# A transformer block with modulated layer norms: first loads in another order, low parts of h from a fused product, six weight slices prepared sooner

## The chip, the cores and the metric

The kernel runs on one core of one Trainium2 chip. A core has five engines that each work through their own instructions in order and wait for each other by semaphores: TensorE (PE in the profile; PEld is its weight load), VectorE (DVE), ScalarE (ACT), GpSimd (POOL) and SyncE (SP), which here only issues DMA transfers. The metric is the device time of one execution in microseconds (us).

## The reference

x is 2048 rows of 512 numbers. A conditioning vector c gives six vectors by one product; the block is attention with 32 heads of 16, then a dense layer with the Mish activation, each behind a layer norm that is scaled and shifted by such vectors.

```python
mod = (_silu(c) @ w_mod).reshape(c.shape[0], 6, 1, -1)
sa, ca, ga, sb, cb, gb = (mod[:, 0], mod[:, 1], ...)
h = _layernorm(x, axis=-1) * (1 + ca) + sa
x = x + ga * _A_ref(h, A_wqkv, A_wo)      # qkv, softmax(q k^T * 16**-0.5) v, @ wo
h = _layernorm(x, axis=-1) * (1 + cb) + sb
x = x + gb * _B_ref(h, B_w1, B_b1, B_w2)  # (h @ w1 + b1) -> mish -> @ w2
```

All is float32. The kernel gets this precision from products in a rounded format (fp32r): it splits each operand into a high part, which is its rounded copy, and a low part, which is what the rounding left, and adds three products: high by high, high by low, low by high.

## The kernel before, in words

**Stages.** In the first stage (about 50 us) the rows of x are read in 16 tiles of 128 rows, four of them a block (`tb`, 512 rows). Each tile is normalised, transposed by TensorE, and scaled and shifted by the columns `modc` into h, kept as `h_h` (high) and `h_l` (low). For each block the first slice of keys (128 columns, eight heads) is computed and put into DRAM, for block 0 that of the queries too, and for blocks 0 and 1 four of the 16 tiles of values. In the second stage (20 steps with t below 0, `PRO`) TensorE computes the maxima of the scores of the first iteration, with further units of q, k and v between them. The attention loop follows: 32 iterations of 16 steps. The last block of the dense layer closes the program.

**What sets the order.** The code is written in the order in which each engine is to work; nothing reorders it. Work that belongs to no step is hung on half-steps: `at(h, f)` runs f at half-step h, where step t has the half-steps 2t and 2t + 1, so that h = -40 is the first. All loads and puts go through SP's queue in that order.

**The first loads.** SP issues c, then the two parts of w_mod that are needed at once (1 MB each: columns for sa and ca), then x tiles 0 to 3, a key and a query slice of `wqkv`, x tiles 4 to 7, a value slice, the other x tiles. Meanwhile GpSimd fills tiles: `sel`, `vq`, `zer`, the five `qa`, and `ka[0]` and `ka[1]`, whose rows of ones stay beside the keys.

**The modulation.** `sil` = c / (1 + exp(-c)) is computed in four small steps, on ScalarE and VectorE. Eight products of `sil` with w_mod (L449) give four partial rows for each of sa and ca in one PSUM bank, which ScalarE copies (L453); 16 products with `sel` (L455) add the partial rows and turn them into columns. VectorE writes them to `modc` (L463, L464).

**The first block's norm.** `first_norm` has VectorE compute statistics of four tiles (L395, L396) and GpSimd the scales in two pairs (L397 to L400). `first_apply` normalises tiles 0 to 2 on ScalarE (L418), 3 on VectorE (L420). `split_hi` and `split_lo` split the first key and query slices.

**A block's h.** `tr_tb` transposes (L435; for block 0 `first_tr`, L427), and for each of four parts k of 128 columns ScalarE writes `h_h` from PSUM (L440), VectorE computes the same value unrounded into `hf` (L441) and `h_l` is hf less h_h (`lo_sub`, L101): on VectorE for the k in `LOV[tb]`, on GpSimd for the others. `stats_tb` and `apply_tb` are the norm of later blocks (L374 to L385). `hi_copy` and `lo_sub` (L94 to L101) are helpers, so many splits share these lines.

**The early weight slices.** `early_prep` loads one of 14 slices of w1 into `ep`, splits it on GpSimd (L98, L101) and puts both parts into `w1scr` in DRAM, for six of the slices in the second stage. They are read in the dense layers.

## Time and profile before

| | us |
|---|---|
| median of 3 runs | 1690.67 |
| lowest, highest run | 1689.92, 1690.83 |
| the profiled execution | 1691.02 |
| its span, first to last instruction | 1689.2 |
| first stage, to the first maxima (L553) | 50.3 |
| second stage, 20 steps, to the first step of the loop (L588) | 51.5 |
| from there to the end of the span | 1587.3 |

TensorE's granted clock is 1.00 on the mean. The busy time of an engine is an average over stages with different limits: the table's first rows concern 50 of 1689 us, and how the engines share them is read from the timeline of that stretch. A row of the chain of waits has a start, a length and what the time went to. A row of the timeline has a start, a length, the engine, the line, the operation, what it writes and reads, and in brackets how long the engine was idle before it and who released it. `x4` means four instructions in one row.

### The profile page before, as it was taken

How to read it: one execution, taken by the hardware profiler on the slowest of the kernel's cores; microseconds unless marked ns; L12 is line 12 of the kernel's file. 1: busy time of each engine (PE TensorE's matmuls, PEld its weight loads, DVE VectorE, ACT ScalarE, POOL GpSimd, SP SyncE). 2: the span in 40 equal slices, each digit the busy share in tenths (PEclk: the TensorE clock that was granted, in tenths of full speed). 3: DMA queues.
4: the chain of work that ended last, by engine and by line, in shares of the span. 5: the costliest groups of instructions: out<-in, count | busy, mean ns of one | idle time of the engine just before them, and what ended most of it. 6: DMA issues, size and time to landing. Idle time of an engine off the chain costs nothing.

```text
span 1689.2 us, 33772 instructions
## 1 busy us (share of the span) xinstructions
PE 1667.3 (99%) x12418; PEld 921.5 (55%) x12418; DVE 1441.5 (85%) x2369; ACT 1355.1 (80%) x2612; POOL 821.1 (49%) x843
## 2 busy tenths in 40 slices
PE   7999999999999999999999999999999999999999
PEld 5755655555444455555555455555555455555687
DVE  8898888888989988888889888888889888883377
ACT  6257777777778998888888998888888998889674
POOL 7555224655313564556323564556323565555442
PEclk9999999999999999999999999999999999999999
DMA  7877556777755443434355434534354533533261
GB/s 248 269 244 199 147 150 185 218 223 216 231 142 146 110 94 98 117 88 129 84 137 152 115 77 93 139 77 127 87 144 122 130 94 77 144 107 132 75 230 63
DMA packets 115406, 238.98 MB, mean 141 GB/s; under 512 B 24928, under 2 KB 50544, under 8 KB 109288
## 3 DMA queue, kind: packets, MB, share of 16 engines
q1 hardware_dynamic: 115240, 236.82, 49.9%
q8 instruction: 98, 1.61, 0.4%
q14 instruction: 68, 0.56, 0.1%
HBM read 180.48 MB, written 51.45 MB: 137 GB/s over the span
## 4 chain that ended last, share of the span: by engine, by line
PE 91%; DVE 3%; ACT 3%; DMA 2%; POOL 1%; issue 1%; SPq 0%; ACTq 0%; DVEq 0%; POOLq 0%
PE bk L606 29%; PE ring L588 22%; PE ring L539 20%; PE bk L139 11%; PE bk L132 3%; PE ring L1219 2%; PE ring L132 2%; DVE mx L541 2%; ACT pr L591 1%; PE ring L553 0%; DMA qa<-mt 0%; DMA xt<-in_A_x 0%; PE ring L922 0%; DMA kscr<-qh 0%; PE ring L568 0%
## 5 line engine op out<-in xcount | busy, mean ns | idle before, releaser
L541 DVE TENSOR_REDUCE mx<-ring 128x1 f32<-128x512 f32 x1968 | 1223.1, 682 | 150.0 <-PE ring L539 136.4
L591 ACT ACTIVATE pr<-ring 128x512 f32<-128x512 f32 x2048 | 1078.4, 603 | 207.1 <-PE bk L139 124.7
L539 PE MATMUL ring<-ka,qa 64*128 64x512 f32 x1968 | 817.9, 429 | 1.4 <-ACT pr L591 1.1
L588 PE MATMUL ring<-qa,ka 64*128 64x512 f32 x2048 | 759.1, 402 | 3.4 <-ACT pr L591 1.9
L606 PE MATMUL bk<-pr,vg 128*32 128x512 f32 x4096 | 545.1, 604 | 0.0
L539 PEld LDWEIGHTS ring<-ka,qa 64*128 64x128 f32 x1968 | 350.5, 184 | 326.2 <-DVE mx L541 251.3
L588 PEld LDWEIGHTS ring<-qa,ka 64*128 64x128 f32 x2048 | 373.7, 184 | 194.7 <-DVE mx L541 111.4
L139 PE MATMUL bk<-h,w 64*128 64x512 f32 (+1 forms) x1080 | 278.1, 390 | 0.0
L139 PE MATMUL bk<-w,a_h 64*128 64x512 f32 x632 | 210.9, 413 | 0.0
L139 PEld LDWEIGHTS bk<-h,w 64*128 64x128 f32 x1080 | 178.5, 184 | 9.3 <-ACT pr L591 1.5
L606 PEld LDWEIGHTS bk<-pr,vg 128*32 128x32 f32 x4096 | 81.2, 108 | 135.4 <-issue 126.0
L139 PE MATMUL bk<-w,a_l 64*128 64x512 f32 x316 | 124.0, 392 | 0.0
L139 PEld LDWEIGHTS bk<-w,a_h 64*128 64x128 f32 x632 | 106.8, 184 | 4.3 <-ACT hb L800 1.0
L978 POOL TENSOR_TENSOR y<-yd,y 128x512 f32<-128x512 f32 x44 | 56.9, 1293 | 89.0 <-ACT yd L977 79.7
L812 POOL TENSOR_SCALAR qq<-ee 128x512 f32<-128x512 f32 x25 | 15.5, 619 | 169.6 <-ACT ee L806 169.6
L828 POOL TENSOR_TENSOR qq<-qq,rr 128x512 f32<-128x512 f32 x42 | 54.1, 1289 | 85.9 <-ACT rr L822 85.9
L814 POOL TENSOR_TENSOR hb<-hb,ee 128x512 f32<-128x512 f32 x42 | 54.1, 1288 | 79.6 <-DVE ee L810 77.7
L139 PE MATMUL bk<-w,o_hl 64*128 64x512 f32 x288 | 79.1, 405 | 0.0
L101 POOL TENSOR_TENSOR a_l<-hb,a_h 128x512 fp32r<-128x512 f32 x53 | 73.1, 1379 | 4.4
L98 POOL TENSOR_SCALAR qh<-qf 128x512 fp32r<-128x512 f32 x27 | 16.7, 619 | 90.8 <-ACT qf L262 69.4
L139 PEld LDWEIGHTS bk<-w,a_l 64*128 64x128 f32 x316 | 58.3, 185 | 3.4
L139 PE MATMUL bk<-h_h,wl 64*128 64x512 f32 x168 | 57.2, 420 | 0.2 <-ACT pr L591 0.2
(219 smaller groups left out, 1909.1 us busy)
## 6 DMA issues: line engine op xcount, KB each, us to landing
ka<-kscr SPq DMA_DIRECT2D x124, 384.0 KB
w<-w2scr SPq DMA_DIRECT2D x56, 512.0 KB
w<-w1scr SPq DMA_DIRECT2D x46, 512.0 KB
vg<-vscr SPq DMA_DIRECT2D x32, 552.0 KB
qa<-qscr SPq DMA_DIRECT2D x124, 100.0 KB
kscr<-qh SPq DMA_DIRECT2D x16, 512.0 KB
qscr<-qh SPq DMA_DIRECT2D x32, 256.0 KB
w2scr<-hl SPq DMA_DIRECT2D x14, 512.0 KB
```

Source lines behind the costliest of these rows:

```text
L101: (nc.gpsimd if eng == "p" else nc.vector).tensor_sub(lo, src, hi.bitcast(F32))
L132: nc.tensor.matmul(acc, l, r, start=start, stop=stop)
L139: i = nc.tensor.matmul(acc, l[64 * g:64 * g + 64], r[64 * g:64 * g + 64], start=start and not then, stop=bool(stop and then))
L539: nc.tensor.matmul(pm, qt[64 * s:64 * s + 64, qs * P:(qs + 1) * P], kt[64 * s:64 * s + 64, kb * TB:(kb + 1) * TB], start=True, stop=True)
L541: nc.vector.tensor_reduce(out=mxs[n][:, s, 4 * j + qs, kb:kb + 1], in_=pm, op=ALU.max, axis=AX.X)
L588: nc.tensor.matmul(p_, kt[64 * s:64 * s + 64, kc * P:(kc + 1) * P], qt[64 * s:64 * s + 64, :], start=True, stop=True)
L591: e = nc.scalar.activation(pr, p_, AF.Exp, scale=SCALE)
L606: nc.tensor.matmul(accs[n][32 * h:32 * h + 32, :], vgs[n][:, o:o + 32], pts.pop((t, h)), start=(kc == 0), stop=(kc == 15))
L814: (nc.vector if tail else nc.gpsimd).tensor_mul(hb, hb, ee)
L828: nc.gpsimd.tensor_mul(qq, qq, rr)
L978: nc.gpsimd.tensor_add(y[i], yd, y[i])
L1219: nc.tensor.matmul(po[i // 2][:, i % 2, :], l[:, s], w[:, r, :], start=(f == 0 and j == 0), stop=(f == FT - 1 and j == 2))
```

## The change

**First loads.** c is loaded through ScalarE's queue. On SP the x tiles 0 to 3 come first, then the first part of w_mod in four tiles of 128 rows, the key slice, the second part in four tiles, the query slice, and the rest as before. SP's queue before (`wma` is w_mod, `xt` a tile of x, `wr` a slice of wqkv):

```order
L332 DMA cc_129<-in_c 128x4x1
L342 DMA wma0_131<-in_w_mod 128x4x512
L342 DMA wma1_132<-in_w_mod 128x4x512
L337 DMA xt_135<-in_A_x 128x512
L337 DMA xt_137<-in_A_x 128x512
L337 DMA xt_139<-in_A_x 128x512
L337 DMA xt_141<-in_A_x 128x512
L234 DMA wr_143<-in_A_wqkv 128x4x128
```

and now:

```order
L333 DMA xt_133<-in_A_x 128x512
L333 DMA xt_135<-in_A_x 128x512
L333 DMA xt_137<-in_A_x 128x512
L333 DMA xt_139<-in_A_x 128x512
L340 DMA wma00_125<-in_w_mod 128x512
L340 DMA wma01_126<-in_w_mod 128x512
L340 DMA wma02_127<-in_w_mod 128x512
L340 DMA wma03_128<-in_w_mod 128x512
L232 DMA wr_145<-in_A_wqkv 128x4x128
L340 DMA wma10_129<-in_w_mod 128x512
```

The x tiles stand ahead of all of w_mod, and the key slice between its two parts.

**Fills, sums and spare transposes.** `sel` is gone; ScalarE fills `ka` from a column of ones. The sums over w_mod are accumulated in PSUM over the four parts of c (`mod_sums`), the row is copied by VectorE and one transpose makes the columns (`mod_cols`). `keep_busy` issues transposes of the identity whose result nobody reads: 40 at the start, 6, 2 after each of four sums, and 4. The norm of the first eight tiles goes by pairs (`stats_two`); tile 3 is normalised by GpSimd.

**Low parts of h.** `hf` is now one fused operation, PSUM times the scale less h_h, and `h_l` is hf plus the shift column. In block 0, VectorE makes the low parts of k = 2 and 3 in place of k = 1. VectorE's instructions before, from the last statistic of block 1:

```order
L375 BN_AGGR ln_mv_246<-ln_st 128x2
L441 TENSOR_SCALAR hf<-ring,modc 128x512
L441 TENSOR_SCALAR hf<-bk,modc 128x512
L101 TENSOR_TENSOR h_l<-hf,h_h 128x512
L441 TENSOR_SCALAR hf<-ring,modc 128x512
L441 TENSOR_SCALAR hf<-bk,modc 128x512
L374 BN_STATS ln_st<-xt 128x6
```

and now:

```order
L401 BN_AGGR ln_mv_359<-ln_st 128x2
L459 SCALAR_TENSOR_TENSOR hf<-ring,modc,h_h 128x512
L459 SCALAR_TENSOR_TENSOR hf<-bk,modc,h_h 128x512
L459 SCALAR_TENSOR_TENSOR hf<-ring,modc,h_h 128x512
L462 TENSOR_SCALAR h_l<-hf,modc 128x512
L459 SCALAR_TENSOR_TENSOR hf<-bk,modc,h_h 128x512
L462 TENSOR_SCALAR h_l<-hf,modc 128x512
L99 TENSOR_TENSOR wl<-wr,wh 128x1024
L381 BN_STATS ln_st<-xt 128x6
```

Two low parts stand there in place of one, and the value slice's low part (`wl`), which came after the four statistics of block 2, comes ahead of them.

**Early slices.** The six slices start at half-steps -39, -37 to -29 in place of -37, -34 to -22; each is split 4 half-steps after its load in place of 7, and put 7 after in place of 10. GpSimd before (`ep` a slice, `wl` the low part of a weight slice, `qh` the high part of a query unit):

```order
L98 TENSOR_SCALAR ep_791<-ep_790 128x512
L101 TENSOR_TENSOR ep_790<-ep_790,ep_791 128x512
L101 TENSOR_TENSOR wl_915<-wr_639,wh_914 128x512
L98 TENSOR_SCALAR ep_827<-ep_826 128x512
L101 TENSOR_TENSOR ep_826<-ep_826,ep_827 128x512
L98 TENSOR_SCALAR qh_945<-qf_947 128x512
```

and now:

```order
L96 TENSOR_SCALAR ep_817<-ep_816 128x512
L99 TENSOR_TENSOR ep_816<-ep_816,ep_817 128x512
L96 TENSOR_SCALAR ep_846<-ep_845 128x512
L99 TENSOR_TENSOR ep_845<-ep_845,ep_846 128x512
L96 TENSOR_SCALAR ep_878<-ep_877 128x512
L99 TENSOR_TENSOR ep_877<-ep_877,ep_878 128x512
L99 TENSOR_TENSOR wl_1014<-wr_728,wh_1013 128x512
```

All six splits now stand ahead of that weight slice's low part; before, it came after four.

The diff, cut to its core:

```diff
-    LOV = ((1,), (), (1, 3), (1, 3))
+    LOV = ((2, 3), (), (1, 3), (1, 3))
...
+    cc = cst.tile([P, DK], F32, name="cc")
+    nc.scalar.dma_start(cc, c.rearrange("o (k p) -> p (o k)", p=P))
...
+        wma = [[lp.tile([P, D], F32, name=f"wma{i}{k}") for k in range(DK)] for i in range(2)]
+        def load_mod(i):
+            for k in range(DK):
+                nc.sync.dma_start(wma[i][k], w_mod[k * P:(k + 1) * P, i * D:(i + 1) * D])
...
         for t in range(4):
             load_x(t)
+        load_mod(0)
         slice_load(1, 0, lp, lp)
+        load_mod(1)
         slice_load(0, 0, lp, lp)
...
-        for i in range(2):
-            nc.gpsimd.memset(ka[i].bitcast(F32), 1.0)
+        hi_copy("a", ka[0], ones.to_broadcast([P, S]))
...
+        def keep_busy(n):
+            for _ in range(n):
+                nc.tensor.transpose(spare[:, :P], ident, ident)
+        keep_busy(40)
...
+        def mod_sums(i, ks):
+            for k in ks:
+                for m in range(DK):
+                    nc.tensor.matmul(prs[i][32 * m:32 * m + 32, :P], sil[:, k:k + 1].to_broadcast([P, 32]),
+                                     wma[i][k][:, m * P:(m + 1) * P], start=(k == 0), stop=(k == DK - 1))
...
+        def mod_cols(i):
+            row = lp.tile([P, P], F32, name=f"row{i}")
+            nc.vector.tensor_copy(row, prs[i][:, :P])
+            nc.tensor.transpose(prs[i][:, P:2 * P], row, ident)
+            cols = prs[i][:, P:2 * P:32]
...
-                nc.vector.tensor_scalar(hf, pt, modc[:, 1, k:k + 1], modc[:, 0, k:k + 1], op0=ALU.mult, op1=ALU.add)
-                lo_sub("v" if k in LOV[tb] else "p", h_l[:, k, s], hf, h_h[:, k, s])
+                nc.vector.scalar_tensor_tensor(hf, pt, modc[:, 1, k:k + 1], h_h[:, k, s].bitcast(F32), op0=ALU.mult,
+                                               op1=ALU.subtract)
+                if k in LOV[tb]:
+                    nc.vector.tensor_scalar_add(h_l[:, k, s], hf, modc[:, 0, k:k + 1])
+                else:
+                    nc.gpsimd.tensor_add(h_l[:, k, s], hf, modc[:, 0, k:k + 1].to_broadcast([P, TB]))
...
+        for q in range(2):
+            stats_two(q)
+        first_apply(3, "p")
+        mod_sums(0, (0, 1))
+        keep_busy(6)
+        first_apply(0)
+        first_tr(0)
+        mod_sums(0, (2,))
+        first_apply(1)
+        first_tr(1)
+        mod_sums(0, (3,))
+        first_apply(2)
+        first_tr(2)
+        first_tr(3)
+        mod_cols(0)
+        hi_k = split_hi(1, 0, "a")
+        split_lo(1, 0, hi_k, "v")
+        for k in range(DK):
+            mod_sums(1, (k,))
+            keep_busy(2)
+        mod_cols(1)
+        keep_busy(4)
+        hi_q = split_hi(0, 0, "p")
+        split_lo(0, 0, hi_q, "p")
+        for q in range(2, 4):
+            stats_two(q)
+        tr_tb(0, pts=pts)
+        for i in range(4, 8):
+            first_apply(i)
+            if i == 5:
+                slice_split(2, 0, eng="v")
...
-        at(h + 7, split)
-        at(h + 10, put)
+        at(h + 4, split)
+        at(h + 7, put)
...
-        at(3 * i - 37, lambda i=i: early_prep(i, 3 * i - 37))
+        at(2 * i - 39, lambda i=i: early_prep(i, 2 * i - 39))
```

102 lines of the change are left out of this document (33 added, 69 removed).

## The prediction

> **What bounds the kernel now.** I read the page first, then the chain of waits in order of time, then the timeline of the first 52 us engine by engine. The page's busy row and its shares of the chain:
>
> ```profile
> PE 1667.3 (99%) x12418; PEld 921.5 (55%) x12418; DVE 1441.5 (85%) x2369; ACT 1355.1 (80%) x2612; POOL 821.1 (49%) x843
> PE 91%; DVE 3%; ACT 3%; DMA 2%; POOL 1%; issue 1%; SPq 0%; ACTq 0%; DVEq 0%; POOLq 0%
> ```
>
> TensorE carries 91% of the chain. Nothing in the diff changes the attention loop's own instructions, so a gain can only be a shift: the loop starts sooner and the rest follows at the same pace. The chain shows where the start is not TensorE's (start us, us, what):
>
> ```profile
> 2.31 7.47 DMA xt<-in_A_x
> ...
> 9.79 0.70 DVE ln_st L395
> ...
> 22.95 2.22 ACT xt L385 x3
> ...
> 38.04 4.52 PE ring L132 x29
> ...
> 48.72 1.15 DVE h_l L101
> ...
> 49.91 0.50 PE ring L132
> ...
> 51.07 1.86 PE bk L132 x14
> ```
>
> Up to 9.8 us the program waits for the first row tiles of x; until 23 us it is VectorE, GpSimd and ScalarE that prepare block 0 and 1; from 30 to 45 us ScalarE and TensorE take turns, and VectorE's last low part at 49.87 lets TensorE go. At 50.4 the maxima of the scores begin. From there to the loop's first step (50.34 to 101.88), busy time by engine:
>
> ```profile
> 50.34:101.88 51.54, 51.42 (x299) 36.64 (x298) 47.57 (x44) 9.84 (x22) 29.74 (x28) 1.00 0.88 280
> ```
>
> TensorE is busy 51.42 of 51.54 us there. So I ask one question: how much sooner does that stretch begin?
>
> **The change part by part. First, the start.** Rows of the timeline (start, us, engine, line, operation), and one of the table of stages (GB/s at the end):
>
> ```profile
> 1.52 0.48 POOL L78 MEMSET sel<- 1x1 f32 x4
> ...
> 3.17 0.20 ACT L361 ACTIVATE sil_e<-cc 128x4 f32<-128x4 f32 x1 [1.18 <-DMA cc<-in_c]
> 3.41 5.33 DVE L362 TENSOR_SCALAR sil_e<-sil_e 128x4 f32<-128x4 f32 x1 [1.76 <-ACT sil_e L361]
> 5.16 3.56 POOL L358 MEMSET ka<- 128x2048 f32 x2
> ...
> 14.82 0.60 ACT L94 CAST wh<-wr 128x512 fp32r<-128x512 f32 x1
> ...
> 25.07 1.04 ACT L94 CAST wh<-wr 128x1024 fp32r<-128x1024 f32 x1
> ```
> ```profile
> 4.00:5.00 1.00, 0.00 (x0) 0.00 (x0) 1.00 (x1) 0.00 (x0) 1.00 (x3) 1.00 1.04 406
> ```
>
> VectorE's addition for the SiLU takes 5.33 us on 512 numbers: it ends at 8.74, just as GpSimd's fills end at 8.72. The change takes the two ka fills (3.56) and the sel fills (0.48) off GpSimd, so its fills end near 4.7. ScalarE fills ka instead; by 0.60 for 512 columns and 1.04 for 1024, 2048 cost 0.60 + 3 x 0.44 = 1.9. ScalarE was free at 1.99 (3.17 less 1.18); with the issue of c ahead of it (some 0.4) the exponential runs near 4.4. The addition, the reciprocal and the product then end near 5.2.
>
> The x tiles now go first. At 406 GB/s four tiles (1.05 MB) take 2.6 us instead of following 2.1 MB of w_mod (5.2 us); x0 is there near 4.1 and x3 near 6.0. So the statistics, which stand behind the SiLU on VectorE, begin at 5.25 instead of 9.79. The steps behind them:
>
> ```profile
> 11.59 0.19 POOL L397 TENSOR_SCALAR ln_rs<-ln_mv 128x2 f32<-128x2 f32 x1 [2.88 <-DVE ln_mv L396]
> ...
> 12.81 0.19 POOL L400 TENSOR_TENSOR ln_rs<-ln_rs 128x2 f32<-128x2 f32 x1
> ```
>
> A pair's scales take 1.41 (11.59 to 13.00), four statistics 3.2 to 3.3 (below: 16.66 to 19.88), one normalisation about 0.8. Second pair: 5.25 + 3.3 + 0.1 + 1.41 = 10.1, normalised 10.9.
>
> TensorE then has eight transposes, four groups of sums for 1 + ca with two spare transposes each, and one transpose of the sums. Its rows, cold and warm:
>
> ```profile
> 9.21 3.64 PE L449 MATMUL ring<-wma,sil 128*32 128x512 f32 x16 [9.21 <-DVE sil L364]
> ...
> 17.11 0.42 PE L427 MATMUL ring<-ident,xt 128*128 128x128 f32 x1
> ...
> 20.98 0.63 PE L132 MATMUL ring<-h_h,wl 128*128 128x512 f32 x1
> ...
> 22.84 0.39 PE L132 MATMUL ring<-h_h,wl 128*128 128x512 f32 x1
> ...
> 25.39 0.60 PE L435 MATMUL bk<-ident,xt 128*128 128x128 f32 x4
> ```
>
> The same product takes 0.63 at 20.98 and 0.39 at 22.84, a transpose follows the next after 0.21 at 17 us and after 0.11 at 25: TensorE runs at half pace until about 21.5. Before, eight products of 512 columns took 3.64, 0.455 each; a group of four with 128 columns is one such, 0.455 cold and 0.23 warm. I take warm, because 40 spare transposes fill it from 1.4 us on. Eight transposes end at 12.0, four times 0.23 + 0.22 makes 13.9, and the copy, the transpose and the addition (0.25, 0.3, 0.15, each between two neighbours of its size) and their hand-overs make 14.75. By then all of w_mod that is needed has landed: 3.4 MB at 406 GB/s from 2.9, and 0.5 to be seen, is 11.8. Before, VectorE was past that point at 16.66: **1.9 sooner**.
>
> **Then VectorE**, whose next 11 us have no gap before:
>
> ```profile
> 16.66 0.68 DVE L374 BATCH_NORM_STATS2 ln_st<-xt 128x6 f32<-128x512 f32 x1
> ...
> 19.88 0.81 DVE L441 TENSOR_SCALAR hf<-ring,modc 128x512 f32<-128x512 f32 x1
> 20.61 0.80 DVE L441 TENSOR_SCALAR hf<-bk,modc 128x512 f32<-128x512 f32 x1
> ...
> 26.70 1.21 DVE L101 TENSOR_TENSOR wl<-wr,wh 128x1024 fp32r<-128x1024 f32 x1
> 27.82 0.81 DVE L441 TENSOR_SCALAR hf<-ring,modc 128x512 f32<-128x512 f32 x1
> ...
> 29.26 1.28 DVE L101 TENSOR_TENSOR ql<-ring,qh 128x512 fp32r<-128x512 f32 x2
> ```
>
> Before: 27.82 - 16.66 = 11.16 to block 1's first hf. Now the same statistics twice (2 x 3.22), the weight's low part (1.12), four fused products and two low parts in place of one. A fused product reads PSUM and SBUF as ql does: between 0.62 (1.28 for two) and 0.73 (hf to hf); I take 0.62, the row with its operands, 2.5 for four. The new low part, an addition of one tensor with a column, has one relative, the normalisation on VectorE:
>
> ```profile
> 15.04 2.68 POOL L101 TENSOR_TENSOR wl<-wr,wh 128x512 fp32r<-128x512 f32 x2
> 15.12 1.48 DVE L420 TENSOR_SCALAR xt<-xt,ln_rs 128x512 f32<-128x512 f32 x1 [2.03 <-POOL ln_rs L400]
> ```
> ```profile
> L101 DVE TENSOR_TENSOR h_l<-hf,h_h 128x512 fp32r<-128x512 f32 x5 | 5.8, 1167 | 0.2
> ```
>
> It ended at 16.60, 0.2 after the first of GpSimd's two operations (15.04 + 1.34): about 0.25 of its own and a wait to the end of what GpSimd has begun. So it costs 0.25 to 1.5, and the subtraction that it replaces 0.69 to 1.17 (the mean). GpSimd works on the low parts of k = 0 and 1 at that time; not knowing to 0.5 us where in a 1.3 us operation VectorE asks, I take half of it: 2 x (0.25 + 0.65) = 1.8. Sum 6.44 + 1.12 + 2.5 + 1.8 = 11.86, so block 1's first hf comes at 26.6, 1.2 sooner.
>
> [...] Both waits taken to the operation's end on my schedule (0.85 and 0.8 rather than 0.65) would be an estimate of 1688.4 for the whole.
>
> **Then GpSimd**, whose four low parts of block 1 TensorE needs:
>
> ```profile
> 29.43 5.06 POOL L101 TENSOR_TENSOR h_l<-hf,h_h 128x512 fp32r<-128x512 f32 x4
> ...
> 34.79 1.18 PE L132 MATMUL ring<-h_l,wh 128*128 128x512 f32 x4
> ...
> 35.28 0.19 POOL L376 TENSOR_SCALAR ln_rs<-ln_mv 128x4 f32<-128x4 f32 x1 [0.79 <-DVE ln_mv L375]
> ...
> 36.94 1.27 POOL L101 TENSOR_TENSOR h_l<-hf,h_h 128x512 fp32r<-128x512 f32 x1
> ```
>
> Scales 1.7 (35.28 to 36.94), four low parts 5.06. An addition with a column spread over 512 has no row; between the 0.62 of a one-tensor operation on GpSimd's queue and these 1.27, I take 1.27, the same two-operand form. 26.6 + 0.1 + 1.7 + 5.06 = 33.5. Before it was 34.49, and TensorE came only at 34.79. Now TensorE comes first: ScalarE's normalisations of x4 to x7 end near 21.9 (was 25.2), the transposes and late products follow, and by the old distances TensorE stands there at 32.4. It gets the last part at 33.5 and ends at 34.0 instead of 35.97: **1.95 sooner**. ScalarE and TensorE then alternate as before (38.04 becomes 36.1).
>
> **The last block.**
>
> ```profile
> 48.04 1.26 POOL L101 TENSOR_TENSOR h_l<-hf,h_h 128x512 fp32r<-128x512 f32 x1 [1.95 <-DVE hf L441]
> ```
>
> The last low part ended at 49.87, 0.57 after GpSimd's at 49.30. The new one ends 0.25 after it, which saves 0.3; the same on k = 1 saves 0.3 ahead of it, and faster products 0.15: **0.75**. Sum 1.95 + 0.75 = 2.7.
>
> **The early slices** cost nothing by my count: GpSimd is busy 29.74 of 51.54 in that stretch, six pairs at 1.9 us are the same work, and TensorE is full. What is queued behind them now is GpSimd's split of the next weight slice, and on SP the puts stand ahead of the next q and k loads; if that cover went, a pair of 1.9 us would show. The low bound is a gain of 0.3, since TensorE's idle time there is 0.12 and a little follows at the first steps.
>
> Sum against the profiled execution: 1691.02, of which the span is 1689.2; its median of the runs shown is 1690.67, 0.35 below. 1690.67 - 2.7 = **1688.0**.
>
> **The rivals.** *VectorE isn't held up.* If the additions slip in between GpSimd's operations, 1.3 goes from VectorE's sum; the low parts of block 1 are there at 32.2, before TensorE, which ends at 33.2 (2.8 sooner), and the last block saves 1.5. 1690.67 - 4.3 = 1686.4. For it: GpSimd has gaps while it waits for hf. Against: the 1.48.
>
> *TensorE stays cold* (the slower side). Spare transposes decide this: if they don't bring it to full pace, every step ahead of the sums doubles. From 1.4: 40 x 0.21 = 8.5 makes 9.9; two groups 0.9, six spare 1.3, sixteen transposes 3.4, two groups 0.9 make 16.4; four times 0.455 + 0.43 and the last copy, 0.8, make 20.7 against my 14.75. That is 5.95 lost: 1690.67 - 2.7 + 5.95 = 1693.9. It turns the sign from 17.45 on. For it: after 3.64 us of products from 9.21, TensorE was still cold at 17. Against: it became warm 1.5 us after the transposes of 16 to 20, and those themselves run at 0.11 later. [...]
>
> *The shift is swallowed.* Two transfers stand in the chain later:
>
> ```profile
> 92.58 7.33 DMA kscr<-qh
> ...
> 372.63 7.70 DMA qa<-mt
> ```
>
> If the loop were paced by such round trips and not by what precedes them, the time stays 1690.7. Against: both are issued by steps that move along with TensorE.
>
> **How the numbers follow.** Forecast 0.43, unhindered VectorE 0.31, cold TensorE 0.15, swallowed 0.11. The forecast's own range is 1686.9 to 1689.6 (waits of 0 to 1.3, fused products of 0.62 to 0.73, the first sums half a microsecond either way). The 8-in-10 range reaches down through the first rival and up past the third, 1684.3 to 1691.3, and leaves the cold case out. A measurement of this kernel tells 0.2% (3.4 us) from no change. Faster by more: 0.9 of the first rival and a quarter of the forecast, 0.38. Slower by more: under half of the cold case and a little for a swallowed shift with a stalled queue, 0.09. The rest 0.53.
>
> **What would show it.** Right: statistics begin near 5.3, the second mod column is added near 14.8, VectorE's first hf of block 1 near 26.6, GpSimd's fourth low part of block 1 near 33.5, the first maxima near 47.6, and the loop's first step about 51.5 later. Transposes at 0.42 after 9 us would show the cold case; low parts of 0.3 on VectorE the unhindered one; a first maximum that is early with an unchanged end, the third. The prediction is wrong if the stretch from the first maximum to the end changes by more than 1 us, for then the early slices or a transfer matter.

## The result, and the profile after

| | before | the change |
|---|---|---|
| median of 22 runs each, one chip | 1690.82 us | 1693.47 us |
| range | 1689.63 to 1692.64 | 1690.08 to 1697.86 |
| profiled execution, its span | 1691.02, 1689.2 | 1691.61, 1689.8 |

The change is slower: ratio 1.0014, 95% interval 1.0009 to 1.0020. On another chip it had 1693.20 (1690.30 to 1695.65) against 1691.13, ratio 1.0013 (1.0004 to 1.0021). The prediction was 1688.0, in a range up to 1691.3. The runs of the change spread over 7.8 us, those of before over 3.0, and its profiled execution is one of the quicker of its runs: it shows where time is lost, but not all of it. This holds for every profile below, each of which is one run: those of e1 and e14 are the slowest of their eleven runs, that of e6 the second slowest, that of e18 the quickest.

The busy row of the change's page reads as before's did. What differs are the shares of the chain of waits (before: TensorE 91%, DMA 2%):

```profile
PE 89%; DMA 4%; ACT 2%; DVE 2%; issue 1%; POOL 1%; SPq 0%; ACTq 0%; POOLq 0%; DVEq 0%
```

So I looked for a mark that comes once in every iteration: VectorE's `mt`, the shift rows, made when an iteration's maxima are complete. Its start in the timeline of each kernel, less its start in the kernel before, tells by how much the program is ahead or behind. First, second and last of 32, before and then the change:

```profile
94.28 0.33 DVE L571 SCALAR_TENSOR_TENSOR mt<-mh,lows,ring 32x128 fp32r<-32x128 f32 x1
139.47 0.34 DVE L571 SCALAR_TENSOR_TENSOR mt<-mh,lows,ring 32x128 fp32r<-32x128 f32 x1 [0.41 <-ACT mh L570]
...
1536.94 0.33 DVE L571 SCALAR_TENSOR_TENSOR mt<-mh,lows,ring 32x128 fp32r<-32x128 f32 x1 [2.63 <-ACT mh L570]
```
```profile
93.27 0.33 DVE L598 SCALAR_TENSOR_TENSOR mt<-mh,lows,ring 32x128 fp32r<-32x128 f32 x1
141.11 0.34 DVE L598 SCALAR_TENSOR_TENSOR mt<-mh,lows,ring 32x128 fp32r<-32x128 f32 x1 [0.42 <-ACT mh L597]
...
1537.38 0.34 DVE L598 SCALAR_TENSOR_TENSOR mt<-mh,lows,ring 32x128 fp32r<-32x128 f32 x1 [2.65 <-ACT mh L597]
```

The change is 1.01 us ahead at the first mark and 1.64 behind at the second: 2.65 us are lost within one iteration, the loop's first. From then on the distance stays, with one step of 1.27 at the eighth mark (it is at 0.1 to 0.5 from there, and 0.44 at the last). That step is not the change's doing: TensorE waits 1.24 us for `qa<-mt` at 380.46 in the profiled run of before and not in that of the change, and of two profiled runs of one and the same kernel below, one has this wait (1.28) and the other has not. I call the distance to before the *offset*, and its value from the second mark to the seventh is the measure of what a kernel does at the loop's entry; the eighth and later ones carry such chance events.

Two questions follow. Why is the first mark only 1.0 us ahead, where 2.7 was forecast? And what takes 2.65 us at the entry?

**The start.** The first part goes as forecast, if 0.8 us late (the second column at 15.56). Then ScalarE, in the timeline of the change, stops in the middle of block 0's four high parts, and TensorE with it:

```profile
16.44 0.77 ACT L458 ACTIVATE h_h<-bk,modc 128x512 fp32r<-128x512 f32 x1
19.73 0.78 ACT L458 ACTIVATE h_h<-ring,modc 128x512 fp32r<-128x512 f32 x1 [2.52 <-DVE hf L459]
...
23.43 1.52 ACT L421 ACTIVATE xt<-xt,ln_rs 128x512 f32<-128x512 f32 x2
```
```profile
20.56 0.73 PE L130 MATMUL ring<-h_h,wh 128*128 128x512 f32 x2 [2.31 <-ACT h_h L458]
...
35.14 1.17 PE L130 MATMUL ring<-h_l,wh 128*128 128x512 f32 x4
...
48.62 0.79 PE L130 MATMUL ring<-h_l,wh 128*128 128x512 f32 x2 [0.16 <-POOL h_l L464]
49.33 0.73 PE L580 MATMUL ring<-ka,qa 64*128 64x512 f32 x4
```

The high part of k = 2 waits 2.52 us for VectorE's fused product of k = 0. It needs nothing from it: the one writes its own columns of h_h, the other reads other columns. Before, this row (20.41) followed the one at 19.75 without a gap. With that wait, TensorE is back at 35.14 for the low parts of block 1, where before it was there at 34.79: the whole of block 0 and 1's gain is gone. From there on 1.36 us are won: 0.87 as the wait for the last low part shrinks from 1.03 to 0.16, 0.26 in the products behind it (0.79 instead of 1.05), the rest in the blocks between. So the first maxima come at 49.33 against 50.34.

**The entry.** TensorE's waits there, in the timeline, before and then the change:

```profile
104.68 0.49 PE L139 MATMUL bk<-h_h,wh 64*128 64x512 f32 x1 [0.40 <-ACT pr L591]
...
107.03 0.50 PE L139 MATMUL bk<-h_h,wl 64*128 64x512 f32 x1 [0.22 <-ACT pr L591]
```
```profile
102.21 0.46 PE L615 MATMUL ring<-qa,ka 64*128 64x512 f32 x1 [1.22 <-DMA qa<-mt]
...
104.87 0.50 PE L566 MATMUL ring<-ka,qa 64*128 64x512 f32 x1 [1.22 <-ACT pr L618]
...
106.34 0.50 PE L137 MATMUL bk<-h_h,wh 64*128 64x512 f32 x1 [0.51 <-ACT pr L618]
...
108.69 0.49 PE L137 MATMUL bk<-h_h,wl 64*128 64x512 f32 x1 [0.24 <-ACT pr L618]
```

3.19 us instead of 0.62: the difference, 2.57, is nearly all of the 2.65 that the offset loses. Where these waits come from is in the chain of waits of the change between 60 and 104 us (start us, us, what):

```profile
62.77 3.64 DMA ep<-in_B_w
...
71.69 4.81 DMA ep<-in_B_w
...
78.14 6.41 DMA qa<-qscr
...
85.28 8.41 DMA qscr<-qh
...
93.87 0.63 POOL qh L96
94.52 7.04 DMA kscr<-qh
...
101.71 0.63 POOL qh L96
102.41 1.30 POOL ql L99
...
103.73 0.02 ACT qf L260
```

It reads from top to bottom: the early slices' loads (between the two shown, GpSimd's splits of slices, 66.49 to 71.06), the third pair's loads of qa and ka behind them in SP's order, the puts of q behind these, GpSimd's next `qh`, which waits (6.84 us ahead of 93.87) until a put has freed one of its two buffers, the put of k, the next `qh` and `ql`, and ScalarE's `qf`, which has one buffer and stands ahead of the first exponentials. TensorE is busy nearly all the time until 101 us, but it isn't in this chain: a second, parallel chain of transfers has become the longer one. In SP's queue the puts of q are issued at 84.62 (before: 82.15) and the four shift-row transfers `qa<-mt` at 96.89 (94.67), although mt is there 1.0 us sooner.

That chain begins long before. In the first stage SP puts a block's k into kscr and loads it back for the first two pairs; the loads read what the puts wrote and wait until it has landed, and the next block's put stands behind them. The first and last of the four rounds of loads and the first slice, in SP's queue before and then in the change:

```profile
39.46 1.76 SPq L322 DMA_DIRECT2D ka<-kscr  x4
...
58.59 1.99 SPq L322 DMA_DIRECT2D ka<-kscr  x4
...
61.19 1.54 SPq L1458 DMA_DIRECT2D ep<-in_B_w  x3
```
```profile
40.42 1.82 SPq L320 DMA_DIRECT2D ka<-kscr  x4
...
60.46 1.73 SPq L320 DMA_DIRECT2D ka<-kscr  x4
62.23 0.43 SPq L232 DMA_DIRECT2D wr<-in_A_wqkv  x1
62.77 2.08 SPq L1485 DMA_DIRECT2D ep<-in_B_w  x4
```

A round takes 6 to 7 us, and what SP waits for ahead of the change's rounds of loads is `kscr<-qh` and `kscr<-ql` (10.5 us in four waits), never TensorE. SP's chain is 0.96 us later than before at its first round and 1.6 at the first slice, while TensorE is 1.0 us sooner. The two chains have moved apart by 2.6 us, and at the entry, where they meet, the later one counts. Not all of this is the change's doing: e3 and e4 below, which are one program up to that point, issue their first round at 40.24 and 38.54. What lies behind the first slice goes with the number of slices. From there to q's puts SP takes 20.96 us before, 21.85 in the change, and 20.4 to 22.7 in every profile with six slices; in those of the changed start with five (below) it takes 18.5 to 19.4.

### The profile page after: what moved, and what is told of

Its sections match the earlier page's. It is cut to its first block, busy times and chain, and to the rows that moved or that the text cites. A ratio compares the mean times of both kernels' runs of the same rounds, so it can differ in the third digit from the quotient of the medians.

```text
span 1689.8 us, 33955 instructions
## 1 busy us (share of the span) xinstructions
PE 1671.9 (99%) x12510; PEld 925.3 (55%) x12510; DVE 1432.7 (85%) x2372; ACT 1357.9 (80%) x2612; POOL 813.7 (48%) x839
## 4 chain that ended last, share of the span: by engine, by line
PE 89%; DMA 4%; ACT 2%; DVE 2%; issue 1%; POOL 1%; SPq 0%; ACTq 0%; POOLq 0%; DVEq 0%
PE bk L633 29%; PE ring L615 22%; PE ring L566 20%; PE bk L137 10%; PE ring L130 2%; PE ring L1246 2%; PE bk L130 2%; DVE mx L568 2%; ACT pr L618 1%; DMA qscr<-qh 1%; DMA xt<-in_A_x 1%; DMA ep<-in_B_w 0%; PE ring L949 0%; DMA kscr<-qh 0%; DMA qa<-qscr 0%
```

## The experiments

None of these kernels leaves out a part of the result. Each was timed beside the kernel before. "Offset" is as above: at the first mark, and from the second on.

**One part alone, and one part undone.** Theory A at this point: the close early slices delay q's and k's puts, and this is the loss. Theory B: the false wait is. First the slices back at their old half-steps in the change, and the slices alone moved in the kernel before:

```diff
 e1_old_slices (from the change)
-        at(h + 4, split)
-        at(h + 7, put)
+        at(h + 7, split)
+        at(h + 10, put)
...
-        at(2 * i - 39, lambda i=i: early_prep(i, 2 * i - 39))
+        at(3 * i - 37, lambda i=i: early_prep(i, 3 * i - 37))
 e2_only_slices: the reverse, in the kernel before
```

> The changed kernel with the early slices back at their old half-steps (load -37, -34 to -22, split 7 and put 10 later); the first stage stays changed. Theory A, the early slices lose it (SP's queue and the transfers run late, and the loop's first steps wait for the row maxima's transfer and for ScalarE behind GpSimd's low parts): the first maxima stay at 49.4, the loop starts near 100.9 without a wait, the first iteration is back to 45.2 to 45.5, and the time is 1 us below before: 1689.8. Theory B, the first stage loses it and the early slices are neutral as forecast: 1693.5.

> The kernel before with the early slices alone moved as in the change. Theory A: the first maxima stay at 50.3, the loop's first steps wait by some 2.5 to 3.5 us, 1693.3 to 1694.3. Theory B: 1690.8, nothing moves.

Measured: e1 1691.55, ratio 0.9999 (0.9990 to 1.0007), offset -0.9 and then +3.5 in the profiled run; e2 1691.60, ratio 1.0000 (0.9992 to 1.0009), offset +0.07 and +0.05. Moving the slices alone costs nothing, so A in this form falls. In the change their place does count: by the medians e1 is level with before, where the change is slower (1.0014, 1.0009 to 1.0020). The profiled run of e1, which loses even more at the entry than the change, doesn't speak against this: it is the slowest of e1's runs, 2.4 us above their median, and its clock fell at the entry, as shown below. B isn't shown either, since in e1 the median comes back to that of before with the false wait in it.

Now the false wait. The function that takes waits away between operations on different PSUM banks leaves a pair alone when one of the two writes a tile, told by its name, that the other touches. The fused product reads h_h, so it now falls under that rule. The edit compares the columns for h_h:

```diff
...
+        def apart(i, j):
+            w, r = spans(i, True), spans(j, False) + spans(j, True)
+            if w and r and all(a1 <= b0 or b1 <= a0 for a0, a1 in w for b0, b1 in r):
+                return {h_h.tensor.name}
+            return set()
...
-                    if j.engine != i.engine and not banks & b and not names & theirs and not made & others:
+                    if j.engine != i.engine and not banks & b and not names & theirs and not made & others - apart(i, j):
```

`spans` gives the columns of h_h that an instruction reads or writes. e3 is the change with this, e4 is e3 with the slices' old half-steps.

> The changed kernel, but ScalarE's high part of k no longer waits for VectorE's fused product of another k (they touch different columns of h; the wait comes from the program's bookkeeping). Theory A with a false wait in block 0: the high part of k = 2 comes at 17.1 in place of 19.7, the first maxima 1 to 1.5 us sooner, near 48.2; the loop's start still waits for transfers, so the time changes by less than 1 us: 1692.5 to 1693.5. Theory B, the false wait is the loss: 1690.5 or less.

> Old places of the early slices and no false wait, the first stage otherwise as changed. Theory A with a false wait: first maxima near 48.2, a shift that arrives at the end: 1688.5. If the false wait is hidden by other waits: 1689.8 as in the first run. Theory B: 1690.5 to 1693.5, by what the false wait is worth.

Measured: first maxima at 46.94 in both (49.33 in the change), 2.4 us sooner and sooner than any of the theories had it. The times: e3 1692.82, ratio 1.0008 (0.9999 to 1.0016); e4 1692.16, ratio 1.0005 (0.9996 to 1.0013). Offsets: e3 -2.3, then +3.5 to +3.9; e4 -3.4, then -0.1 to +0.3. So a start that is 3.4 us sooner reaches the loop and is gone after its first iteration. Both theories fall; what eats the gain is the entry, and it eats more where more arrives. SP's chain has hardly moved in e4: its last round of loads is issued at 58.68, the first slice at 60.96, where before had 58.59 and 61.19. TensorE's rows in e4:

```profile
99.19 0.47 PE L630 MATMUL ring<-qa,ka 64*128 64x512 f32 x1 [0.65 <-DMA qa<-mt]
...
101.85 0.50 PE L581 MATMUL ring<-ka,qa 64*128 64x512 f32 x1 [1.24 <-ACT pr L633]
...
103.32 0.79 PE L137 MATMUL bk<-h_h,wh 64*128 64x512 f32 x1 [0.49 <-ACT pr L633]
```

The waits sum to 2.38, 1.76 more than before, but 3.3 us were lost. The rest shows in the last row: a product that takes 0.49 elsewhere takes 0.79, and the granted clock (the third number from the end of a row of stages) is below 1 after the waits. In e1's profiled run it falls to half:

```profile
95.00:100.00 5.00, 5.00 (x24) 3.11 (x23) 4.34 (x4) 1.17 (x2) 3.28 (x4) 1.00 0.91 289
100.00:105.00 5.00, 3.09 (x17) 1.81 (x15) 2.92 (x5) 1.15 (x3) 1.90 (x2) 0.85 0.95 306
105.00:110.00 5.00, 4.71 (x18) 3.31 (x19) 3.12 (x5) 2.80 (x6) 1.88 (x2) 0.50 0.98 309
```

In e4 it is 0.83 from 100 to 110 us, 1.7 us at full pace, which is about the missing part.

Theory C from here on: the entry is paced by the transfers of the stretch before it (SP's order, and a memory path whose DMA share in before is 0.85 to 1.09 in each stage of 5 us from 65 to 110 us); before is just balanced there, and TensorE that comes sooner waits, and may lose its clock as well.

**What the fused product is worth.** This run undoes it in the change, which also takes the false wait away, as the product reads h_h no longer:

```diff
-                nc.vector.scalar_tensor_tensor(hf, pt, modc[:, 1, k:k + 1], h_h[:, k, s].bitcast(F32), op0=ALU.mult,
-                                               op1=ALU.subtract)
-                if k in LOV[tb]:
...
+                nc.vector.tensor_scalar(hf, pt, modc[:, 1, k:k + 1], modc[:, 0, k:k + 1], op0=ALU.mult, op1=ALU.add)
+                lo_sub("v" if k in LOV[tb] else "p", h_l[:, k, s], hf, h_h[:, k, s])
```

> The change with the low parts of h made as before (VectorE's product with scale and shift, then the difference by VectorE or GpSimd over the whole tile), the other parts of the change kept, six close slices too. The pair is no longer dependent by name, so the false wait is gone as well. If the fused product is worth the 1.2 us that the prediction gave it: first maxima (a 64x512 group of TensorE) at 48.1, against 46.9 with it and without the false wait. If VectorE was not the bound of this stage: 46.9 to 47.2. The median, swallowed at the entry as in e3_no_false_wait: 1691.5 to 1693.

Measured: first maxima at 49.95, against 50.34 before, 49.33 in the change and 46.94 in e3. The forecast was 48.1: without its wait the fused product is worth 3.0 us at this place and not 1.2, with the wait 0.6, and all else in the new start 0.4. (These are single profiled runs; the first marks of e13 and e16, whose first stage is the same, lie 1.6 us apart, as the clock fell in one of them.) The median, 1693.18, ratio 1.0012 (1.0003 to 1.0021), with an offset of -0.4 and then +1.1 to +1.6: a start that is only 0.4 us sooner, with six close slices, is slower than before like the change. Its first slice is issued at 63.24, later than in the change (62.77). The false wait is then not what makes the change slower.

**Waits and transfers at the entry.** Four kernels: the fourth pair's loads behind the shift rows; two early slices in place of six; a wait made longer in the kernel before; and the first two together.

```diff
 e6_pair_later (from e4_both)
-    for pp, h in ((2, -22), (3, -8)):
+    for pp, h in ((2, -22), (3, -4)):
 e8_two_early (from e4_both)
-    EARLY = 6
+    EARLY = 2
 e9_before_stalled (from the kernel before)
+    def stall():
+        for _ in range(2):
+            nc.scalar.copy(gates[0], ka[0][:, :TB].bitcast(F32))
+    at(0, stall)
 e10_two_early_pair_later: e6 and e8 together
```

> The kernel without the false wait and with the early slices at their old half-steps (e4_both), with the loads of the fourth pair of heads' qa and ka issued four half-steps later, behind the first shift rows (qa<-mt). Theory C (the loop's entry is paced by transfers: puts of k and q that land late, in SP's order and on a full memory path): the four qa<-mt issues move up by some 3 us on SP (92 to 93 us there becomes about 90), the wait of a first score product for qa<-mt goes, the wait for ScalarE's first exponentials behind the last qf stays; the time falls by at most 1 us against e4_both, to about 1691.3. Rival D (the order on SP alone is what swallows the shift): both waits go and the 3.4 us of the first maxima arrive, 1688.0.

> e4_both with two early weight slices in place of six, so that four loads of 256 KB and eight puts of 256 KB are taken out of the stretch from 62 to 92 us and prepared with the others later. Theory C (full memory path and SP's order before the loop): the puts of q and k land sooner, GpSimd's waits for qscr<-qh and kscr<-qh at 89 and 98 us (4.9 and 3.0 us in e4_both) fall below 2 us, ScalarE's last qf stands no longer late ahead of the first exponentials, TensorE's waits at 99 and 102 us go with the drop of its clock, and the end of the third group of maxima (233 us in before, 233 in e4_both, by the shift-row product of VectorE) comes at about 230; the time is 1688 unless the four slices that are prepared later hold up the weights' end, which would show at the end and not at the entry. Rival E (the entry is bound by ScalarE's own work and not by transfers): the waits stay, and the time stays at 1692.

> The kernel before with two added copies on ScalarE (128x512, about 0.55 us each, into a tile that is not yet in use) ahead of its last qf before the loop: a wait at the loop's entry is made 1.1 us longer and nothing else is changed. If a wait costs what it lasts: 1692.0, the granted clock stays at 1.0 and the runs spread as those of before. Theory C's second half (a wait of TensorE above about a microsecond at this place lets its clock fall by half for some microseconds): granted clock below 0.9 in a 5 us window between 100 and 115 us in the profiled run or a spread of the runs up to 1697, and a median of 1693 to 1694.

> e8_two_early with the fourth pair's loads behind the first shift rows as in e6_pair_later. Theory C: both waits at the entry are gone, no granted clock below 1 between 95 and 115 us, 1687.5 to 1688, the fastest of all. If D holds alone: as e6_pair_later. If E holds: 1692.

Measured, with the kernel before at 1691.89:

| | median | ratio | offset, first mark | from the second on | last |
|---|---|---|---|---|---|
| e6 | 1691.51 | 0.9998 (0.9988 to 1.0007) | -3.5 | +0.7 to +1.0 | +3.2 |
| e8 | 1713.99 | 1.0127 (1.0113 to 1.0141) | -3.2 | -3.3 to -3.0 | -3.4 |
| e9 | 1690.28 | 0.9989 (0.9980 to 0.9998) | -0.1 | +0.9 | -0.8 |
| e10 | 1716.88 | 1.0148 (1.0133 to 1.0164) | -1.4 | -0.1 to +0.3 | +0.6 |

e8 answers the question of the entry: with four slices' traffic gone, the 3.2 us pass through it whole. TensorE's only waits there are 0.39 and 0.23. What it loses, it loses behind the loop: its last mark is 3.4 us ahead of before and its span is 22.9 us longer (1712.1). Slices that are prepared later leave work for the end: TensorE waits 10.83 us for GpSimd's `a_h` at 1604.89, where before has no wait. How this comes about I didn't follow. e10 is a miss. It was to be the fastest of all; its first mark is only 1.4 us ahead (granted clock 0.93 and 0.73 from 20 to 30 us), a wait of 1.21 for `vg<-vscr` at 108.78 takes nearly all of that, and it ends later still than e8.

e6 moved a wait instead of taking it away. The wait for `qa<-mt` is gone, and the fourth pair's loads now stand ahead of the values:

```profile
108.29 1.94 PE L648 MATMUL bk<-pr,vg 128*32 128x512 f32 x8 [2.03 <-DMA vg<-vscr]
```

The granted clock is 0.79 and 0.86 in the two stages from 105 us. (This profiled run is 2.9 us above e6's median.) e9 is a miss for the second half of theory C: a stall of ScalarE by 1.1 us moved the program by 0.9, in pieces of 0.27, 0.65 and 0.50, with the clock at 1.0 throughout, and the median didn't rise at all. So pieces of that size cost what they lasted in this run. Why the median then came out 0.1% below before's, these runs don't tell; the 0.9 us are within what the later chance waits give and take.

**The order mended, with six slices.**

```diff
 e11_pair_behind_v (from e4_both): the fourth pair behind the values' load
-    for pp, h in ((2, -22), (3, -8)):
+    for pp, h in ((2, -22), (3, -2)):
 e12_dense_reordered (from e3_no_false_wait)
-    for pp, h in ((2, -22), (3, -8)):
+    for pp, h in ((2, -28), (3, -2)):
```

> e4_both with the fourth pair's loads of qa and ka issued behind load_v (half-step -2 in place of -8; in e6_pair_later they stood ahead of vg<-vscr, which came 2.0 us late for the first 128x32 products). Theory C: the qa<-mt wait (0.65 us in e4_both) and the vg<-vscr wait (2.03 in e6_pair_later) are both gone, the waits for ScalarE's pr are at most 0.5 each as in e6_pair_later, and the offset of VectorE's shift-row product mt from that of before, -3.4 at the first, is between -3 and -2 from the second on (e4_both -0.1, e6_pair_later +0.7); the profiled run then ends 2 to 3 us under before's 1689.2 span, less what the run's later waits differ by (about 1.2 each). If the transfers are bound by the path and not by SP's order: offset still about 0, 1691 to 1692.

> e3_no_false_wait (the change's six early slices close together, no false wait) with the third pair's loads six half-steps sooner (ahead of the last four slices' puts in SP's order) and the fourth pair's behind load_v. Theory C: the slices' traffic is over by about 82 us, q's and k's puts behind it are no longer held up by the third pair's loads, offset of mt -2 to -3 from the second on (e3_no_false_wait -2.3 at the first and +3.5 at the second); median 1688 to 1689. If the close slices themselves delay q's split on GpSimd: offset stays above 0, 1691 or more.

Measured: e11 1689.63, ratio 0.9989 (0.9980 to 0.9997), offset -3.1, then -1.7 and -0.8; e12 1692.74, ratio 1.0008 (0.9999 to 1.0017), offset -1.3, then +1.2 to +1.4. In e11 the waits for transfers are gone, as forecast, but only a quarter of the gain stays (-0.8, where -3 to -2 was forecast). In e12 they aren't: 1.15 for ScalarE's exponentials and 0.34 for the values. SP's order is a part of the matter with the old spacing; with the close slices it isn't enough.

**One slice fewer.** e13 is e4 with `EARLY = 5`, the only edit; e15 does the same to the kernel before, as a control; e14 to the change; e18 to e3; e16 is e13 with e11's order. e19 and e20 are the change and e14 again, side by side on one chip.

> e4_both with five early slices in place of six. e8_two_early kept its 3.3 us at the entry, but 26 us were lost after the loop because four slices were prepared later. Theory C: the offset of mt from the second on is about -1.5 (a quarter of the way between -0.1 with six slices and -3.3 with two, or more if the last slice is the one that collides with q's put). For the end: if the loss behind the loop goes with the slices, 6 us each, 1696; if it has a threshold, 1689.

> The kernel before with five early slices in place of six, the control. Theory C: before is only just balanced at the entry (TensorE waits 0.40 and 0.22 us there), so that one slice fewer gives at most these, offset of mt -0.3 to 0 from the second on, 1690.5 to 1691.5. If one slice fewer is a gain of its own: -2 to -3, 1689, as in e13_five_early.

> The change with five early weight slices in place of six, nothing else. Theory C (the sixth slice's traffic before the loop swallows the sooner start): the offset of mt from that of before, -1.0 at the first and +1.6 from the second on in the change, is -0.5 to -1.0 from the second on, the waits of TensorE for qa<-mt at 102 us go, and the median is 1690 to 1690.5. If the false wait with its low clock is the cause of the loss: offset and median as in the change, 1692 to 1693.5.

> e13_five_early with the fourth pair's loads behind load_v as in e11_pair_behind_v. Theory C: the entry of e13_five_early keeps its 3.2 us already, so the order has little left to give: within 0.5 us of 1689.15; a later vg or fourth pair could cost up to 1 us.

> e3_no_false_wait with five early slices in the change's close placement. Theory C: SP's queue and the memory path are freed of the sixth slice, so the offset of mt (+3.5 from the second on with six) is -1.5 to -3 from the second on, and the median is 1689 to 1690. If the close placement itself delays q's and k's puts: offset above 0, 1691 or more.

> The change, unaltered, beside its five-slice version on one chip. Theory C: 1692 to 1694, runs spread over 4 us or more (low clock after the entry's waits in a part of them).

> The change with five early slices, the same kernel as e14_change_five. Theory C: 1690.5 to 1691, 1.5 to 3 us below e19_change_again, runs spread over less than 3 us. If the earlier difference was one between chips or days: within 0.8 us of e19_change_again.

| | median (range) | ratio to before | offset, first | from the second on | last |
|---|---|---|---|---|---|
| e13: e4, five | 1689.15 (1687.11 to 1691.19) | 0.9987 (0.9979 to 0.9996) | -3.2 | -3.2 to -2.9 | -2.5 |
| e15: before, five | 1692.52 (1690.57 to 1696.26) | 1.0010 (1.0002 to 1.0019) | 0.0 | 0.0 to +0.1 | +1.1 |
| e14: change, five | 1690.84 (1689.72 to 1692.36) | 0.9996 (0.9987 to 1.0005) | -0.5 | -0.3 to +0.2 | +1.0 |
| e16: e13, pair later | 1689.92 (1687.71 to 1695.60) | 0.9988 (0.9979 to 0.9998) | -1.6 | -1.7 to -1.3 | -1.4 |
| e18: e3, five | 1691.05 (1688.53 to 1693.26) | 0.9998 (0.9989 to 1.0007) | -3.3 | -1.7 to -1.6 | -2.8 |
| e19: change | 1693.20 (1690.30 to 1695.65) | 1.0013 (1.0004 to 1.0021) | -0.8 | +1.5 to +1.8 | +1.2 |
| e20: change, five | 1690.69 (1689.48 to 1691.63) | 0.9995 (0.9986 to 1.0004) | -0.6 | -0.3 to +0.1 | -0.3 |

The pair e19 and e20 settles that the sixth slice does it: one chip, one slice of 256 KB fewer, and the change loses 2.5 us of its time. The wait for `qa<-mt` is gone with it, and those for `pr` are at most 0.51. In e20 the chain of waits is TensorE's own until 101 us; in e14, the same program, it still runs through the transfers, so there the two end nearly together. SP's first slice is issued at 63.31 and 63.12 in these two, even later than in the change, and costs nothing. What the slice takes away stays open: with its load go two puts and a split of 1.9 us on GpSimd, and no run parts these. GpSimd is not short of time there: in the change it is busy for 4.45 of the 15 us from 80 to 95 and waits 6.84 us for `qscr<-qh` ahead of 93.87. The stage from 100 to 105 us, of e19 and then of e20 (the second number is TensorE's busy time of the 5 us):

```profile
100.00:105.00 5.00, 2.99 (x18) 1.96 (x18) 3.50 (x5) 1.91 (x4) 1.91 (x2) 1.00 0.80 267
```
```profile
100.00:105.00 5.00, 4.27 (x27) 2.62 (x27) 4.76 (x7) 2.60 (x6) 2.39 (x4) 1.00 1.03 341
```

The control says that this is no gain of its own: before with five slices has the same entry as with six (offset 0.0), and is 0.1% slower in the end. The sixth slice costs nothing where TensorE arrives late enough, and 1.8 us of offset where it arrives half a microsecond to a microsecond sooner.

e13 is faster than before, and its offset was forecast at -1.5: it keeps 2.9 of its 3.2 us through the entry and 2.5 to the last mark, and its only waits at the entry are 0.38 and 0.24. e16 began with less (granted clock 0.87 and 0.79 from 20 to 30 us) but passed nearly all of it on. e18 is half a miss: it passes 1.6 of its 3.3 us, still waits 1.36 us for ScalarE at 101.49, and its median is level with that of before although its profiled run has the shortest span of all, 1686.7. In this run the close placement holds up the entry even with five slices.

## Why the prediction was wrong

*The start up to the second column* (forecast 14.75, measured 15.56). The SiLU addition took 0.17 us instead of 5.33 and the statistics began at 5.06, as forecast (5.25). Late were the four sums with their spare transposes, forecast at 0.45 a round:

```profile
1.34 6.32 PE L363 MATMUL ring<-ident 128*128 128x128 f32 x40 [1.34 <-POOL ident masks.py:199]
...
11.77 0.27 PE L430 MATMUL ring<-ident,xt 128*128 128x128 f32 x1
...
12.19 0.43 PE L435 MATMUL ring<-wma,sil 128*32 128x128 f32 x8
12.54 0.44 PE L363 MATMUL ring<-ident 128*128 128x128 f32 x2
12.91 0.42 PE L435 MATMUL ring<-wma,sil 128*32 128x128 f32 x8
```

A round takes 0.72, from 12.19 to 12.91: 0.35 for the sums and 0.37 for the two spare transposes, priced at 0.23 and 0.22. The sums were priced as one product of 512 columns, and are several small ones; the transposes at 0.11 each, which holds only within a row of them. The rival of a cold TensorE is refuted by the same rows: 40 transposes take 6.32 and not 8.5, and one as above takes 0.27 where the cold ones took 0.42. In the row of 40, TensorE's first work, they follow each other after 0.21 us until 4.81 and after 0.11 from 4.98 on, so TensorE became warm on transposes alone. The 11.8 for the landing of w_mod, with its 0.5 us, was an estimate, and no row measures that term; the four sums show no wait for a transfer.

*VectorE's chain* (block 1's first hf forecast 26.6, measured 27.90). The column came 0.8 late, and 0.55 is a wait for ScalarE's `wh`, which follows from the stop described above. From the column to that hf e3, which has no such stop, takes 11.62 us (15.69 to 27.31), forecast 11.86. Fused products follow each other after 0.64, forecast 0.62. The low parts took 0.50 each in block 0, where 0.25 and half a wait of 1.3 were priced. That model was right, and only its guess of the wait was off: VectorE's addition ends 0.28 us after the GpSimd operation that was running when it began. In the timeline of the change:

```profile
20.51 2.22 POOL L464 TENSOR_TENSOR h_l<-hf,modc 128x512 fp32r<-128x512 f32 x2
22.52 0.49 DVE L462 TENSOR_SCALAR h_l<-hf,modc 128x512 fp32r<-128x512 f32 x1
...
39.42 1.04 POOL L464 TENSOR_TENSOR h_l<-hf,modc 128x512 fp32r<-128x512 f32 x1 [1.62 <-DVE hf L459]
40.03 0.71 DVE L462 TENSOR_SCALAR h_l<-hf,modc 128x512 fp32r<-128x512 f32 x1
```

GpSimd ends at 22.73 and at 40.46, VectorE at 23.01 and at 40.74. All six additions of the change keep this distance (0.28 to 0.29), and so do the six in each profile of e3, e13, e18 and e19. So VectorE's addition ends only behind GpSimd's operation, and the rival in which it isn't held up falls. That it is held up by 0.2 to 0.5 us is an estimate: the 0.49 to 0.83 us that the additions of the change take, less the 0.28 behind GpSimd's end.

*GpSimd's low parts and TensorE behind them* (forecast 33.5, and TensorE done at 34.0). GpSimd's fourth ended at 33.81, its four at 4.04 in place of 5.06. The step that failed is in the same paragraph: "ScalarE's normalisations of x4 to x7 end near 21.9". They ended at 24.95, because ScalarE had stood still for 2.52 us ahead of them, and TensorE came to the low parts at 35.14 instead of 32.4. In e3, without that wait, they end at 22.84 and TensorE is done with the block at 33.92, where 34.0 was forecast. That the two agree is in part luck: in e3 the first hf still comes 0.7 later than forecast, GpSimd's four operations are 1.0 shorter, and TensorE, there at 32.75, shows no wait for them. So the sum of 1.95 came out for a program that the change isn't: I looked at what the fused product costs VectorE, and not at who has to wait for an operation that now reads h_h.

*The last block* (0.75 forecast): the wait of 1.03 fell to 0.16, and the first maxima came 1.0 sooner. *First maxima* at 49.33, forecast 47.6; 46.94 without the false wait.

*From the first maxima to the loop's first step, "about 51.5 later".* This is the step that turned the sign. The loop's first step came 52.88 later (49.33 to 102.21), and more was lost right behind it. The stage row showed TensorE busy 51.42 of 51.54 us, and I took that for the bound of the stretch. Yet the chain of waits of before, in the same stretch, has left TensorE at 80.8 us and goes through ScalarE, GpSimd, SP and transfers to the end of it:

```profile
80.83 0.60 ACT qf L262
...
92.58 7.33 DMA kscr<-qh
100.05 0.63 POOL qh L98
100.75 1.30 POOL ql L101
```

Both chains were nearly equally long; moving TensorE's forward gains nothing unless the other moves too, and in the change's profile the other is later. The row at 92.58 stood in the prediction, in the rival "the shift is swallowed", and was dismissed because "both are issued by steps that move along with TensorE". They don't: TensorE was 1.0 us sooner, and SP issued q's puts 2.47 later and `qa<-mt` 2.22 later. SP's rounds of put and load run at their own pace, and what is issued waits behind them and the slices. That rival had the mechanism and was given 0.11; it put the time at no change and left only a little chance that it ends slower.

*"The early slices cost nothing by my count."* Right for them alone (e2, ratio 1.0000). Wrong beside a sooner start: what hid them was that TensorE came late enough for q's and k's transfers, not that it was full. The sixth slice is worth 2.5 us of the change's median. The prediction's last sentence named this case: a stretch that changes by over 1 us means that the slices or a transfer matter. In the profiled run of the change it is 1.6 us longer up to the end of the span: by the marks 2.65 are lost at the entry, and 1.27 come back at the eighth mark by the chance wait of before.

What isn't settled: the profiled run of the change lies 1.9 us below its median. Its runs' time and their mean granted clock go against each other (correlation -0.64 over 22 runs, -0.77 in e4, -0.92 in e6, but -0.25 in e20 and 0.09 in e14), and e1 and e4 show the clock falling after the waits at the entry; that the slower runs of the change are those in which this happens is likely, but no profile of such a run was taken. The runs of the change with five slices, which has no wait above 0.51 there, spread over 2.2 us in e20, those of the change beside it over 5.4. Nor is a difference of 0.1% between two medians safe by itself: e9, with a stall added, came out 0.1% faster than before and e15 0.1% slower, and nothing at the entry explains either. What repeats is the offset at the entry, +1.6 and +1.5 in two profiles of the change and -0.3 in both with five slices.

## What to carry to other kernels

A stretch in which one engine is busy 99.8% of the time can still be bound by something else just as much: read the chain of waits in that stretch, and if it runs through transfers, a sooner start of the busy engine may be worth nothing until these are sooner too, as here. Price extra work by what shares its queue and its path, and try it together with the gain that it is to accompany; alone it may look free (here the close slices alone had ratio 1.0000, and the sixth slice cost the change 2.5 us). When a fused operation reads a tile that the old one didn't, look for everyone who writes any part of that tile: a dependency kept by the tile's name took 2.4 of the 3.0 us that the fusion saved here up to the first maxima.

## What the runs showed of the hardware

In some of these runs the granted clock fell after short idle times of TensorE: waits of 1.89 us in e1 and of 0.65, 1.24 and 0.49 in e4 are followed by 5 to 10 us at 0.50 to 0.85, whereas 0.27, 0.65 and 0.50 in e9 are not (1.00 from 95 to 115 us), and 1.22, 1.22 and 0.51 in the profiled run of the change are not either (1.00 from 95 to 115 us). So the length of one wait didn't decide it here. The same happened at the start, in the change after the 2.31 us wait at 20.56 (0.70 from 20 to 25 us), yet not in its second profiled run (e19, 1.00, where TensorE is busy for 3.15 of these 5 us). So the fall varies between runs of one kernel, and no run here shows what decides it. The record of the granted clock doesn't always show the start of a program: in before it reads 1.00 from 15 to 20 us, where transposes follow each other after 0.21, against 0.11 later, and in the change from 1.3 us on, where they follow each other after 0.21 until 4.81.

For `h_l`, GpSimd added a column spread over 512 elements in 1.04 us in nine of ten cases in the change (1.22 in the tenth), where subtracting a full second tensor took it 1.26 to 1.30 in before. VectorE's addition of a scalar column to 128x512, SBUF to SBUF, that began while GpSimd worked ended 0.28 us after GpSimd's operation, in 30 of 30 cases in five profiles; it took 0.49 to 0.83 us in all.
